# One queue for the later units' transfers, and the next unit's decays turned earlier, in a fused RWKV-6 and SiLU kernel

## The chip, the cores and the metric

The kernel runs on one core of a Trainium2 chip. Its time is the device time of one execution in microseconds (us); the runs below give the median of several executions, and the profile shows one execution of its own, engine by engine. The engines are PE (TensorE, with its weight loads as PEld), DVE (VectorE), ACT (ScalarE), POOL (GpSimd) and SP (SyncE, which here only issues transfers). A "q" behind an engine's name (SPq, ACTq) marks its sequencer: waiting, and issuing transfers.

## The reference

Two blocks follow one another. The first is a linear attention with a decay per channel: for each of 4 batches and 8 heads (48 channels each), over 768 steps,

```python
for t in range(S):
    cur = np.einsum('bhd,bhe->bhde', u[None] * kt, vt)
    y[:, :, t] = np.einsum('bhd,bhde->bhe', rt, state + cur)
    state = wt[:, :, :, None] * state + np.einsum('bhd,bhe->bhde', kt, vt)
```

The second takes the result as 3072 tokens of 384 values: `h = x @ w_in` (384 x 2048), `g = h * sigmoid(h)`, `out = g @ w_out` (2048 x 384). Everything is float32.

## The kernel before, in words

**Units.** The sequence is cut into 6 pieces of 128 steps, the batches into 2 pairs: 12 units, numbered 0 to 11, in the order of time. Unit 5 is the sixth. Within a unit the 128 steps are handled by doubling: at level l (0 to 6) neighbouring blocks of 2^l steps are joined. For this `tw[i][l]` holds the products of w over blocks of 2^l steps; `product` (L404) makes the next level from the one before on POOL, `products_of(i, ...)` names several. `grow_keys` (L624, POOL) and `grow_queries` (L618, DVE) multiply keys and queries by such products, `odd_keys` (ACT) copies keys, `prepare` and `go_on` bundle these for a level, and `burst` (L782) lets PE make the scores of two levels at once. The short distances (below 8 steps) are made apart: `block_bonus` multiplies r, k and w as they lie in DRAM (`tokens_rk`, `tokens_w`) on POOL, `block_sum` adds them up on DVE into `block_sums`, `block_move` sends this to DRAM (`kept`) and reads it back in another layout, and `block_turn` and `block_write` put it into the scores.

**Loads.** `load_blocks(i, name, g)` (L118) loads a quarter of r, k or w of unit i into the room `raw` with four transfers of small runs; a unit has 48 of them, 16 for each of r, k and w. From unit 4 on there is one room per name (`slot`, L99), so the next unit's part can only be loaded once `turn` (L347, on DVE a transpose in blocks, L361) has read the room: w, k and r are turned at different places. `load_rk` loads `tokens_rk` (parts 0 and 1) and `tokens_w` (part 2), `load_values` loads v.

**Second block.** It lags behind the first. In turn i of the loop PE works through `downs(i - 2)`, seven quarters of the down projection (`quarter`, L1298; each accumulates 16 rows of matmuls, and its result is read out of PSUM by ACT at L1328 or by DVE at L1331), and `ups(i - 1)`, twenty parts of the up projection (`first_part`, L1189, matmuls at L1180, joined by DVE at L1207 and ACT at L1201, L1204 and L1223). The quarters 0, 2, 4 and 6 share one bank in PSUM, and so do 3 and 5; each must have been read before the next one adds to it. `sums` (L1282, DVE at L1294) makes the sums that the quarters multiply, `sums_of_x` (L1128) those of the input x.

**x.** After `y_state` (L831) and `y_values` PE has the unit's y; ACT copies it to `yt`. `x_out` (L935) sends it to DRAM (`turned`) in two transfers and `x_in` (L942) reads it back in the layout of tokens: on ACT's queue in the loop.

**Order.** Nothing is scheduled automatically: `mix(i)` (L958) writes the order by hand as a list of groups, each with a number of PE steps (from `downs` and `ups`) that follow it. What is emitted first on an engine or a queue runs first, and a waiting instruction holds up all behind it. For i > NPAIR = 4 the order is the one from L1019 on; unit 5 has another place for two bundles (`soon`). The loads of the next unit are added to the groups at the end of `mix` (L1054 to L1059): k and w early, then v and r. In that order `turn` of w stands in group 9 with products 0 to 3, and products 4 to 6 in group 19; for unit 5, w is turned at the end of turn 4 (`turns`) and multiplied at the start of turn 5 (`start`).

Of the kernel before, what the change touches and what calls it, by code (L numbers as in the profile page):

```python
# [8 lines left out]
F32 = mybir.dt.float32  # L9
# [29 lines left out]
def kernel(  # L39
# [11 lines left out]
    nc = tc.nc  # L51
# [3 lines left out]
    L = 128  # L55
    NL = 7
# [3 lines left out]
    Q = NB * NP  # L60
# [8 lines left out]
    NPAIR = 4  # L69
# [333 lines left out]

    def product(i, l, engine=nc.gpsimd):  # L404
        t = tw[i][l]
        up = pt.tile([128, Q, L >> (l + 1)], F32, name=f"tw{l + 1}", bufs=2 if l == NL - 1 else 1)
        engine.tensor_tensor(out=up, in0=t[:, :, 0::2], in1=t[:, :, 1::2], op=ALU.mult)  # L407
        tw[i].append(up)

# [542 lines left out]
    def both(fn, i, *args):  # L952
        return [(fn, i, b, *args) for b in range(NB)]

    def block_loads(i, names="wkr"):
        return [(load_blocks, i, name, g) for name in names for g in range(4)]

    def mix(i):  # L958
# [15 lines left out]
        def start(j):  # L974
            return [*at(j <= NPAIR + 1, *products_of(j, *range(1, NL))), (grow_own, j, 1)]

        def products_of(j, *ls):
            return [(product, j, l) for l in ls]
# [16 lines left out]
        else:  # L995
            j = i - 1
            if i <= NPAIR:
# [15 lines left out]
                          ([], 1),  # L1013
                          ([(burst, i, 5), (keep_level, i, 5, 0), (keep_level, i, 6, 0), (go_on, i, 6), (block_turn, i), (block_write, i, 1)], 2),
                          ([(keep_level, i, 5, 1), (keep_level, i, 6, 1)], 1),
                          ([(block_write, i, 0)], 1),
                          (end[0], 2), (end[1], 0)]
            else:
                soon = i > NPAIR + 1  # L1019
                keys_2 = [(odd_keys, i, 2), (grow_keys, i, 2, False), *at(soon, (grow_queries, i, 2)), *sum_steps(i, 2)]  # L1020
# [22 lines left out]

        if i == NPAIR:
# [5 lines left out]
        if i < NPAIR:  # L1050
            behind = [group for group, _ in groups[8:]]
            for at, group in enumerate(behind):
                group += loads[at * len(loads) // len(behind):(at + 1) * len(loads) // len(behind)]
        elif ahead:  # L1054
            blocks = block_loads(i + 1, "wkr" if i <= NPAIR else "kwr")
            for at, some in ((1, blocks[0:3]), (2, blocks[3:6]), (3, blocks[6:8]), (12, [(load_values, i + 1), *blocks[8:9]]),
                             (13, blocks[9:10]), (14, blocks[10:11]), (15, blocks[11:])) if i > NPAIR else ((0, blocks[0:3]), (1, blocks[3:6]), (2, [*blocks[6:8]]), (3, [(load_values, i + 1)]),
                             (12, blocks[8:9]), (13, blocks[9:10]), (14, blocks[10:11]), (15, blocks[11:])):
                groups[at][0].extend(some)  # L1059
        return groups  # L1060

# [420 lines left out]
```

## Time and profile before

| what | value |
|---|---|
| median of 3 runs | 577.57 us |
| lowest and highest | 576.17 and 579.52 us |
| the profiled execution | 578.62 us, of which the span of the engines is 576.8 |
| mean granted TensorE clock | 0.997 |
| transfers on SP's queue (q1) | 196272 packets, 44.01 MB |
| transfers on ACT's queue (q10) | 10128 packets, 12.39 MB |
| packets below 512 B | 186048 of 206485 |

A row of the timeline reads: start and length in us, engine, line of the kernel, operation, tile written <- tiles read, shape, count; in brackets the idle time of the engine just before it and what ended it. Starts are counted from the start of the span. Rows of the same kind that follow one another are merged.

### The profile page before, as it was taken

Reading aid. Unit: us, or ns where it says so; the run is one execution under the profiler, and the core shown is the slowest. Engines: PE = TensorE matmul, PEld = TensorE weight load, DVE = VectorE, ACT = ScalarE, POOL = GpSimd, SP = SyncE. Lnnn points to the kernel's source line nnn. Section 1 sums busy time; section 2 is a strip of 40 time slices with the busy share of each in tenths; the row PEclk is TensorE's granted clock in tenths of the full one; section 3 lists DMA queues with packets and bytes.
Section 4 is the critical chain, followed back from the end, with each engine's and each line's share of the span. In section 5 each row is a group of like instructions: output and inputs, shape, how many; then the busy total and the mean of one; then the engine's idle time right before and its main releaser. Section 6 shows DMA issues by size and latency. Waiting matters only on the chain.

```text
span 576.8 us, 18839 instructions
## 1 busy us (share of the span) xinstructions
PE 558.9 (97%) x7782; PEld 518.0 (90%) x7782; DVE 482.5 (84%) x748; ACT 270.8 (47%) x604; POOL 394.8 (68%) x447
## 2 busy tenths in 40 slices
PE   8989999999999899899999999999999999999997
PEld 7767777698899899799999999999999999899997
DVE  7979789898899998799799899999888899782250
ACT  5779694432541372273274273274264272371330
POOL 6998868547799997787687697687696687700000
PEclk9999999999999999899999999999999999999999
DMA  9946885345344453554555555555555553102000
GB/s 222 311 74 186 233 248 94 46 65 126 96 87 75 108 86 68 108 90 82 89 110 96 109 83 98 102 96 91 103 87 96 112 89 71 37 4 56 28 8 21
DMA packets 206485, 57.59 MB, mean 100 GB/s; under 512 B 186048, under 2 KB 198208, under 8 KB 206400
## 3 DMA queue, kind: packets, MB, share of 16 engines
q1 hardware_dynamic: 196272, 44.01, 39.4%
q10 hardware_dynamic: 10128, 12.39, 8.3%
q8 instruction: 61, 1.00, 0.8%
q14 instruction: 24, 0.20, 0.1%
HBM read 47.14 MB, written 9.18 MB: 98 GB/s over the span
## 4 chain that ended last, share of the span: by engine, by line
PE 49%; DVE 15%; SPq 13%; DMA 9%; POOL 7%; issue 4%; ACT 2%; ACTq 0%; DVEq 0%; POOLq 0%
PE p_o L1323 14%; SPq L127 11%; PE p_o L1180 11%; PE p_h L1180 7%; PE p_h L1073 4%; PE p_m L1262 4%; DVE temps L1294 3%; PE p_sc L697 2%; POOL tk L639 2%; DMA raw<-in_k_dram 2%; PE p_h L1323 2%; POOL w_in_sb L260 2%; DVE tr L621 2%; DMA kept<-block_sums 2%; DMA raw<-in_r_dram 1%
## 5 line engine op out<-in xcount | busy, mean ns | idle before, releaser
L639 POOL TENSOR_TENSOR tk<-tk,tw 128x256 f32<-128x256 f32 x128 | 105.0, 841 | 18.3 <-ACT tk L609 8.0
L1323 PE MATMUL p_o<-own,temps 128*128 128x192 f32 x528 | 88.8, 327 | 1.2 <-ACT partial L1328 1.1
L1323 PEld LDWEIGHTS p_o<-own,temps 128*128 128x128 f32 x528 | 85.8, 190 | 2.6 <-ACT partial L1328 2.2
L407 POOL TENSOR_TENSOR tw<-tw 128x256 f32<-128x256 f32 (+6 forms) x83 | 45.4, 546 | 48.2 <-DVE tw L361 44.3
L1180 PE MATMUL p_o<-xt,w_in_sb 128*64 128x128 f32 x1152 | 72.3, 273 | 1.0 <-POOL w_in_sb L1119 0.7
L1073 PE MATMUL p_h<-xt,w_in_sb 128*128 128x256 f32 x288 | 66.1, 384 | 1.7 <-POOL w_in_sb L260 1.6
L1323 PE MATMUL p_o<-w_out_sb,gt 128*128 128x192 f32 x340 | 62.1, 337 | 4.3 <-DVE ob L1331 3.5
L1180 PEld LDWEIGHTS p_o<-xt,w_in_sb 128*64 128x64 f32 x1152 | 64.7, 137 | 1.5 <-POOL w_in_sb L1119 0.9
L1073 PEld LDWEIGHTS p_h<-xt,w_in_sb 128*128 128x128 f32 x288 | 53.6, 190 | 10.0 <-POOL w_in_sb L260 2.4
L1323 PEld LDWEIGHTS p_o<-w_out_sb,gt 128*128 128x128 f32 x340 | 56.5, 194 | 6.6 <-DVE ob L1331 5.1
L490 POOL TENSOR_TENSOR ruk<-tokens_rk 128x384 f32<-128x384 f32 x48 | 53.6, 1138 | 4.2 <-DMA tokens_rk<-in_k_dram 4.2
L621 DVE TENSOR_TENSOR tr<-tr,tw 128x512 f32<-128x512 f32 x61 | 54.1, 886 | 0.7
L1328 ACT COPY partial<-p_o 128x192 f32<-128x192 f32 x33 | 10.4, 319 | 80.4 <-PE p_o L1323 43.8
L1294 DVE TENSOR_TENSOR temps<-gt 128x512 f32<-128x512 f32 (+1 forms) x48 | 44.7, 969 | 0.0
L609 ACT COPY tk<-tk 128x256 f32<-128x256 f32 x52 | 20.9, 403 | 38.7 <-POOL tk L639 30.5
L648 POOL TENSOR_TENSOR tk<-tk,tw 128x256 f32<-128x256 f32 x32 | 25.2, 820 | 16.1 <-DVE tk L361 16.1
L1204 ACT ACTIVATE gt<-p_o 128x512 f32<-128x512 f32 x45 | 26.0, 601 | 19.8 <-PE p_o L1180 19.8
L715 DVE COPY_PREDICATED score<-mask,p_sc 128x512 f32<-128x512 int8 x42 | 31.3, 800 | 0.8 <-PE p_sc L697 0.6
L1328 ACT COPY ob<-p_o 128x192 f32<-128x192 f32 x11 | 3.5, 319 | 59.8 <-PE p_o L1323 53.8
L1323 PE MATMUL p_o<-w_out_sb,temps 128*128 128x192 f32 x176 | 30.4, 326 | 0.0
L490 POOL TENSOR_TENSOR spare<-tokens_rk 128x384 f32<-128x384 f32 x24 | 29.0, 1221 | 0.6
L1323 PE MATMUL p_h<-w_out_sb,gt 128*128 128x192 f32 x168 | 29.1, 326 | 0.0
(240 smaller groups left out, 1293.3 us busy)
## 6 DMA issues: line engine op xcount, KB each, us to landing
w_out_sb<-in_moe_w_in_dram SPq DMA_DIRECT2D x6, 768.0 KB, 6.6
w_out_sb<-in_moe_w_out_dram SPq DMA_DIRECT2D x4, 768.0 KB, 5.9
own<-in_moe_w_out_dram SPq DMA_DIRECT2D x4, 768.0 KB, 6.3
tokens_w<-in_w_dram SPq DMA_DIRECT2D x8, 384.0 KB, 4.6
turned<-yt ACTq DMA_DIRECT2D x16, 192.0 KB, 2.6
xt<-turned ACTq DMA_DIRECT2D x8, 384.0 KB, 3.8
tokens_rk<-in_r_dram ACTq DMA_DIRECT2D x7, 384.0 KB, 4.8
tokens_rk<-in_k_dram ACTq DMA_DIRECT2D x7, 384.0 KB, 6.0
```

The source lines that it names most:

```text
L127: nc.sync.dma_start(out=room[(2 * e + a) * 32:(2 * e + a + 1) * 32, :, g, 0:d1 - d0], in_=src[b0:b0 + NB, e::2, t0:t0 + 32, d0:d1].rearran ...
L407: engine.tensor_tensor(out=up, in0=t[:, :, 0::2], in1=t[:, :, 1::2], op=ALU.mult)
L490: mul = lambda out, one, two: nc.gpsimd.tensor_tensor(out=out, in0=one, in1=two, op=ALU.mult)
L621: nc.vector.tensor_tensor(out=odd, in0=odd, in1=tw[i][l][:, :, 0::2][:, :, :, None].to_broadcast([128, Q, L >> (l + 1), c]), op=ALU.mult)
L639: nc.gpsimd.tensor_tensor(out=out, in0=have, in1=odd_products(i, l, b, *blocks), op=ALU.mult)
L648: nc.gpsimd.tensor_tensor(out=have, in0=have, in1=odd_products(i, l, b, [2, NP * ni]), op=ALU.mult)
L715: nc.vector.copy_predicated(out=dst, mask=masks[l][:, :, None].to_broadcast([128, NB, NP, ni, c]), data=sc[e].rearrange("p (b q) (i c) -> ...
L1073: nc.tensor.matmul(p_h[:, a, :], lhsT=w_in_sb[:, c, f * 128:(f + 1) * 128], rhs=xt[i][:, c, :], start=(a == 0 and c == 0), stop=(a == 1 an ...
L1180: nc.tensor.matmul(p[h:h + PD, q, :], lhsT=left[:, f:f + PD], rhs=right, start=first and q == 0, stop=q == 3, skip_group_check=True)
L1204: nc.scalar.activation(out=g(f, t), in_=have, func=AF.Silu)
L1294: nc.vector.tensor_tensor(out=out, in0=one, in1=two, op=op)
L1323: nc.tensor.matmul(p, lhsT=left(f), rhs=right[:, f, :], start=which in (0, 1, 3) and f == 0, stop=f == FH - 1, skip_group_check=True)
```

## The change

For turns 5 to 11 it does four things, and one at the end of turn 4.

1. The transfers of `x_out`, `x_in` and of `tokens_rk`, five in a turn, are issued by SP and no longer by ACT.
2. The block loads are written into the groups: w first (groups 0 and 1, behind `x_out` and `x_in`), k in groups 2 to 4, r in groups 7, 11, 14 and 15, v in group 12. `block_move` is split: `block_sums` is sent out in group 6, ahead of `tokens_rk`, and read back in group 8; `tokens_w` is loaded in group 10.
3. The next unit's w is turned in groups 6 and 8 and no longer in group 9, its products 0 to 2 are made in group 8 ahead of `go_on(i, 4)`, and products 3 to 6 in group 9 behind it, so that none is left in group 19. As this overlaps with products of the unit at work, the odd units put levels 5 and 6 in the rooms `both_b` and `diag0`, whose last use is earlier.
4. Unit 5 gets the order of the others: the bundle `keys_2` (with `grow_queries(i, 2)`) in group 2 and `keys_3` in group 3.
5. For unit 5 w is turned in the last but two group of turn 4, behind `block_write`, and all its products follow in the next group, behind `block_bonus` 0 to 3.

```diff
     def product(i, l, engine=nc.gpsimd):
         t = tw[i][l]
-        up = pt.tile([128, Q, L >> (l + 1)], F32, name=f"tw{l + 1}", bufs=2 if l == NL - 1 else 1)
+        if i > NPAIR and i % 2 and l + 1 in (5, 6):
+            up = pt.tile([128, Q, L >> (l + 1)], F32, name={5: "both_b", 6: "diag0"}[l + 1], bufs=1)
+        else:
+            up = pt.tile([128, Q, L >> (l + 1)], F32, name=f"tw{l + 1}", bufs=2 if l == NL - 1 else 1)
...
-            return [*at(j <= NPAIR + 1, *both(turn, j, "w"), (product, j, 0)), *both(turn, j, "k")]
+            return [*at(j <= NPAIR, *both(turn, j, "w"), (product, j, 0)), *both(turn, j, "k")]
...
-            return [*at(j <= NPAIR + 1, *products_of(j, *range(1, NL))), (grow_own, j, 1)]
+            return [*at(j <= NPAIR, *products_of(j, *range(1, NL))), (grow_own, j, 1)]
...
-                          ([(block_write, i, 0)], 1),
-                          (end[0], 2), (end[1], 0)]
+                          ([(block_write, i, 0), *at(i == NPAIR, *both(turn, i + 1, "w"))], 1),
+                          ([*end[0], *at(i == NPAIR, *products_of(i + 1, *range(NL)))], 2), (end[1], 0)]
...
-                groups = [([*both(turn, i, "r"), (grow_own, i, 0), (x_out, j)], 2),
-                          ([*at(j >= NPAIR, (add_update, j)), *start(i), *bonus_steps(i, 4), (x_in, j), (reverse_v, i)], 1),
-                          ([*at(not soon, (grow_queries, i, 2)), *at(soon, *keys_2)], 1),
-                          ([*at(soon, *keys_3), *at(not soon, *keys_2), (sums_of_x, j, 0, 1)], 1),
-                          ([(sums_of_x, j, 2), *at(not soon, *keys_3), *bonus_steps(i, 6, 7), (sums_of_x, j, 3, 4, 5, 6)], 2),
+                groups = [([*both(turn, i, "r"), (grow_own, i, 0), (x_out, j, nc.sync), *loads("w", 0, 1)], 2),
+                          ([*at(j >= NPAIR, (add_update, j)), *start(i), *bonus_steps(i, 4), (x_in, j, nc.sync), *loads("w", 2, 3), (reverse_v, i)], 1),
+                          ([*keys_2, *loads("k", 0, 1)], 1),
+                          ([*keys_3, (sums_of_x, j, 0, 1), *loads("k", 2)], 1),
+                          ([(sums_of_x, j, 2), *bonus_steps(i, 6, 7), (sums_of_x, j, 3, 4, 5, 6), *loads("k", 3)], 2),
                           ([(burst, i, 3), *sum_steps(i, 3), (keep_level, i, 3), *sum_steps(i, 4)], 2),
-                          ([*at(ahead, (load_rk, i + 1, (0, 1), nc.scalar)), (block_move, i, False), (block_move, i, True), *at(ahead, (load_rk, i + 1, (2,)))], 1),
-                          ([], 1),
-                          ([(keep_level, i, 4)], 2),
-                          ([(go_on, i, 4), *at(ahead, *both(turn, i + 1, "w"), *products_of(i + 1, 0, 1, 2, 3))], 1),
-                          ([], 1),
-                          ([], 1),
-                          ([], 1),
+                          ([(block_move, i, False), *at(ahead, (load_rk, i + 1, (0, 1)), (turn, i + 1, 0, "w"))], 1),
+                          ([*loads("r", 0)], 1),
+                          ([(block_move, i, True), *at(ahead, (turn, i + 1, 1, "w"), *products_of(i + 1, 0, 1, 2)), (keep_level, i, 4)], 2),
+                          ([(go_on, i, 4), *at(ahead, *products_of(i + 1, 3, 4, 5, 6))], 1),
+                          ([*at(ahead, (load_rk, i + 1, (2,)))], 1),
+                          ([*loads("r", 1)], 1),
+                          ([*at(ahead, (load_values, i + 1))], 1),
                           ([(sums_of_x, j, 7)], 1),
-                          ([(prepare, i, 5)], 2),
-                          ([], 1),
+                          ([(prepare, i, 5), *loads("r", 2)], 2),
+                          ([*loads("r", 3)], 1),
...
-                          ([*at(ahead, *bonus_steps(i + 1, 1, 2, 3)), *at(ahead and i > NPAIR, *products_of(i + 1, 4, 5, 6))], 2),
+                          ([*at(ahead, *bonus_steps(i + 1, 1, 2, 3)), ], 2),
```

`loads(name, *gs)` is `[(load_blocks, i + 1, name, g) for g in gs if ahead]`. The block loads at the end of `mix` stay for turn 4 alone.

More of the change, by code (lines that the diff above doesn't have):

```diff
@@ L1015, in mix @@
                           ([(keep_level, i, 5, 1), (keep_level, i, 6, 1)], 1),
-                          ([(block_write, i, 0)], 1),
-                          (end[0], 2), (end[1], 0)]
-            else:
-                soon = i > NPAIR + 1
-                keys_2 = [(odd_keys, i, 2), (grow_keys, i, 2, False), *at(soon, (grow_queries, i, 2)), *sum_steps(i, 2)]
+                          ([(block_write, i, 0), *at(i == NPAIR, *both(turn, i + 1, "w"))], 1),
+                          ([*end[0], *at(i == NPAIR, *products_of(i + 1, *range(NL)))], 2), (end[1], 0)]
+            else:
+                keys_2 = [(odd_keys, i, 2), (grow_keys, i, 2, False), (grow_queries, i, 2), *sum_steps(i, 2)]
@@ L1021, in mix, with loads @@
                 keys_3 = [(prepare, i, 3), *bonus_steps(i, 5)]
-                groups = [([*both(turn, i, "r"), (grow_own, i, 0), (x_out, j)], 2),
-                          ([*at(j >= NPAIR, (add_update, j)), *start(i), *bonus_steps(i, 4), (x_in, j), (reverse_v, i)], 1),
-                          ([*at(not soon, (grow_queries, i, 2)), *at(soon, *keys_2)], 1),
-                          ([*at(soon, *keys_3), *at(not soon, *keys_2), (sums_of_x, j, 0, 1)], 1),
-                          ([(sums_of_x, j, 2), *at(not soon, *keys_3), *bonus_steps(i, 6, 7), (sums_of_x, j, 3, 4, 5, 6)], 2),
-                          ([(burst, i, 3), *sum_steps(i, 3), (keep_level, i, 3), *sum_steps(i, 4)], 2),
-                          ([*at(ahead, (load_rk, i + 1, (0, 1), nc.scalar)), (block_move, i, False), (block_move, i, True), *at(ahead, (load_rk, i + 1, (2,)))], 1),
-                          ([], 1),
-                          ([(keep_level, i, 4)], 2),
-                          ([(go_on, i, 4), *at(ahead, *both(turn, i + 1, "w"), *products_of(i + 1, 0, 1, 2, 3))], 1),
-                          ([], 1),
-                          ([], 1),
-                          ([], 1),
+                def loads(name, *gs):
+                    return [(load_blocks, i + 1, name, g) for g in gs if ahead]
@@ L1054, in mix @@
         elif ahead:
[L1055 to L1058, printed above, removed]
+            blocks = block_loads(i + 1)
+            for at, some in ((0, blocks[0:3]), (1, blocks[3:6]), (2, [*blocks[6:8]]), (3, [(load_values, i + 1)]),
+                             (12, blocks[8:9]), (13, blocks[9:10]), (14, blocks[10:11]), (15, blocks[11:])) if i <= NPAIR else ():
                 groups[at][0].extend(some)
```

## The prediction

> **What bounds the kernel now.** I read the busy line first, then the stretches of the loop, then the idle marks of PE, and last the queues behind them.
>
> ```profile
> span 576.8 us, 18839 instructions
> PE 558.9 (97%) x7782; PEld 518.0 (90%) x7782; DVE 482.5 (84%) x748; ACT 270.8 (47%) x604; POOL 394.8 (68%) x447
> ```
>
> PE is busy 97% of the span, so the prize is small: at most the time in which PE waits. The change touches turns 5 to 11 of the loop over units and the end of turn 4 (the sixth unit is number 5). I cut the span where PE starts y_state of the unit before (the first L840 row of each turn).
>
> ```profile
> 258.47 0.34 PE L840 MATMUL p_m<-tr,state 48*48 48x128 f32 x4
> ```
>
> ```profile
> 210.99:258.47 47.48, 44.65 (x693) 42.97 (x689) 41.44 (x63) 21.00 (x53) 37.69 (x44) 0.96 0.49 87
> 258.47:301.26 42.79, 42.65 (x692) 41.52 (x689) 39.05 (x61) 19.83 (x51) 32.75 (x38) 1.00 0.52 94
> 301.26:344.03 42.77, 42.77 (x692) 41.49 (x688) 39.20 (x61) 20.57 (x52) 33.92 (x38) 1.00 0.53 96
> 344.03:387.67 43.64, 43.01 (x693) 41.47 (x689) 40.91 (x61) 20.43 (x52) 32.30 (x38) 1.00 0.54 99
> 387.67:430.96 43.29, 42.97 (x693) 41.47 (x689) 39.52 (x61) 20.16 (x51) 34.46 (x39) 1.00 0.52 95
> 430.96:473.52 42.56, 42.20 (x677) 40.92 (x673) 37.77 (x60) 20.18 (x52) 30.80 (x37) 1.00 0.54 98
> ```
>
> These are turns 5 to 10: length, then the busy time of PE, PEld, DVE, ACT and POOL. Turns 5 to 9 hold the same matmuls, yet turn 5 is 4.7 us longer, and turn 8 0.9. Inside a turn the place where PE comes late is the last of the seven quarters of the down projection, which may not start before DVE has read an earlier quarter out of PSUM (L1331, `ob`).
>
> ```profile
> 233.41 4.55 PE L1323 MATMUL p_o<-w_out_sb,gt 128*128 128x192 f32 x16 [2.60 <-DVE ob L1331]
> ```
>
> ```profile
> 277.63 2.76 PE L1323 MATMUL p_o<-w_out_sb,gt 128*128 128x192 f32 x16
> ```
>
> ```profile
> 320.66 2.87 PE L1323 MATMUL p_o<-w_out_sb,gt 128*128 128x192 f32 x16
> ```
>
> ```profile
> 364.26 2.87 PE L1323 MATMUL p_o<-w_out_sb,gt 128*128 128x192 f32 x16
> ```
>
> ```profile
> 450.75 2.76 PE L1323 MATMUL p_o<-w_out_sb,gt 128*128 128x192 f32 x16
> ```
>
> ```profile
> 493.05 2.87 PE L1323 MATMUL p_o<-w_out_sb,gt 128*128 128x192 f32 x16 [0.92 <-DVE ob L1331]
> ```
>
> Counted from the start of its turn this quarter starts at 22.42 (turn 5), 19.16 (6), 19.40 (7), 20.23 (8) and 19.79 (10). Turn 6 has it earliest; turn 7 has the shortest rest, 42.77 - 19.40 = 23.37. A turn without any wait would take 19.16 + 23.37 = 42.53 (estimate). Over that lie 0.26 in turn 6, 0.24 in 7, 1.11 in 8, 0.76 in 9; turn 10, with fewer matmuls, is 19.79 - 19.16 = 0.63 late, and turn 11 shows 0.92 of idle. That is 3.9 us in all, and 4.95 more in turn 5.
>
> What makes it late:
>
> ```profile
> 353.49 0.43 PE L1323 MATMUL p_o<-own,temps 128*128 128x192 f32 x1 [0.53 <-ACT partial L1328]
> ```
>
> ```profile
> 309.69 0.32 ACT L1328 COPY partial<-p_o 128x192 f32<-128x192 f32 x1 [3.86 <-DMA raw<-in_r_dram]
> ```
>
> ```profile
> 354.34 1.30 DVE L361 STREAM_TRANSPOSE tr<-raw 128x512 f32<-128x512 f32 x2 [0.96 <-DMA raw<-in_r_dram]
> ```
>
> ```profile
> 441.41 1.30 DVE L361 STREAM_TRANSPOSE tr<-raw 128x512 f32<-128x512 f32 x2 [1.47 <-DMA raw<-in_k_dram]
> ```
>
> First, ACT stands still behind its own transfers (x_out, x_in): in turn 7 it is idle 3.86 us before a copy out of PSUM, in turn 8 such a copy holds PE 0.53. Secondly, DVE waits for the last loads of r: 0.96 in turn 8, 1.47 in turn 10. Both lead to the late quarter.
>
> **The change part by part.**
>
> *r sooner, on SP.* Today SP issues r last:
>
> ```profile
> 297.35 11.45 SPq L127 DMA_DIRECT2D raw<-in_r_dram  x16
> ```
>
> ```profile
> 318.24 8.42 SPq L127 DMA_DIRECT2D raw<-in_w_dram  x16
> ```
>
> ```profile
> 327.72 0.41 SPq L549 DMA_DIRECT2D kept<-block_sums  x1
> 334.27 0.38 SPq L554 DMA_DIRECT2D spare<-kept  x1
> ```
>
> ```profile
> 341.54 8.72 SPq L127 DMA_DIRECT2D raw<-in_r_dram  x12
> ```
>
> ```profile
> 303.46 2.37 ACT L866 COPY yt<-p_m 48x512 f32<-48x512 f32 x4 [0.18 <-PE p_m L861]
> ```
>
> From 328.13 to 334.27 SP stands 6.1 us before the read of `kept`, and r goes behind that. The change puts the loads of tokens_rk and a quarter of r into this hole and splits the rest of r over the turn. At 8.42 / 16 = 0.53 us per load, SP's new order is: x_out once y is copied (305.83, 4.6 us into turn 7), with the loads of w queued behind that wait and behind x_in's wait for `turned`; then w and x_in 9 us, k 8.5, two outputs and `kept` (ready only 26 us in, as now), tokens_rk and r 3, the five reads of `kept` 3, w's tokens, values and the other twelve r 10: the last r is out about 44 us in, against 51 today (twelve by 350.26, four more behind, turn 7 from 301.26). The waits of DVE for r go (estimate: all). SP's added work is five transfers a turn, 5 x 0.53 = 2.6 us. They hide in that hole; if `kept` still lands 6.5 us after its issue, half of the hole stays, and SP loses its slack: the first rival below.
>
> *ACT freed.* x_out, x_in and two loads leave ACT, and with them the waits of its copies. PE's 0.53 in turn 8 goes, and its like in turn 10. x_in now stands behind eight loads of w, about 10 us into the turn; first used by DVE at 318.67 - 301.26 = 17.4:
>
> ```profile
> 318.67 0.81 DVE L1141 TENSOR_TENSOR xt<-xt 128x256 f32<-128x256 f32 x1
> ```
>
> The Trainium skill, "DMA: Bandwidth & Descriptors", section "Issuing engines are not separate DMA queues", speaks against this part: it says that all issuers share the same 16 engines, and that issuing from several only saves issue time, usually small. By it, taking ACT's queue away would only lose issue time; the 3.86 us row above shows a cost of the second queue that the section does not count, so I follow the row.
>
> *w turned in groups 6 and 8, its products ahead of go_on(4).* DVE does the same two transposes earlier, in gaps before L1207. On POOL the products now come before the keys of levels 4 and 5 (the fourth product waits there for DVE's go_on(4), with those keys behind it only from level 5 on; the rooms of both_b and diag0 have no reader left, so they add no wait):
>
> ```profile
> 329.15 1.33 DVE L715 COPY_PREDICATED score<-mask,p_m 128x512 f32<-128x512 int8 x2
> ```
>
> ```profile
> 332.34 2.65 POOL L407 TENSOR_TENSOR tw<-tw 128x512 f32<-128x512 f32 x4 [5.58 <-DVE tw L361]
> 334.95 1.20 POOL L639 TENSOR_TENSOR tk<-tk,tw 128x256 f32<-128x256 f32 x2
> ```
>
> ```profile
> 336.92 0.69 PE L697 MATMUL p_sc<-tr,tk 48*64 48x64 f32 x32
> ```
>
> POOL was idle 5.58 us before the products. The second half of w now takes the place of L715 on DVE and is turned by 329.15 + 0.65 = 329.8, 2.5 us sooner. The seven products (2.65 + 2.06, the latter from the row below) and two pairs of keys (1.20 each) then end by 336.9, today 336.15. PE needs these keys for the second half of its scores, 0.5 us after 336.92. Cost 0, at worst 0.3 a turn. At the end of a turn three products leave POOL,
>
> ```profile
> 346.94 2.06 POOL L407 TENSOR_TENSOR tw<-tw 128x32 f32<-128x32 f32 x3
> ```
>
> 2.06 us beside DVE's sums, which helps turn 11, where no r is awaited.
>
> Turns 6 to 11 together: I take 0.2 + 0.2 + 1.1 + 0.7 + 0.6 + 0.9 = 3.7 of the 3.9; bounds 0 and 3.9.
>
> *The sixth unit.*
>
> ```profile
> 212.09 1.49 DVE L1294 TENSOR_TENSOR temps<-gt 128x512 f32<-128x512 f32 x1
> ```
>
> ```profile
> 219.07 0.69 DVE L1294 TENSOR_TENSOR temps<-gt,temps 128x512 f32<-128x512 f32 x1
> 219.68 1.30 DVE L361 STREAM_TRANSPOSE tw<-raw 128x512 f32<-128x512 f32 x2
> 220.90 1.26 DVE L361 STREAM_TRANSPOSE tk<-raw 128x512 f32<-128x512 f32 x2
> ```
>
> ```profile
> 221.06 1.04 POOL L407 TENSOR_TENSOR tw<-tw 128x512 f32<-128x512 f32 x1 [3.77 <-DVE tw L361]
> ```
>
> ```profile
> 230.69 1.13 DVE L527 TENSOR_REDUCE block_sums<-ruk 128x4 f32<-128x192 f32 x4 [1.85 <-POOL ruk L490]
> ```
>
> ```profile
> 308.64 1.30 DVE L361 STREAM_TRANSPOSE tk<-raw 128x512 f32<-128x512 f32 x2
> ```
>
> ```profile
> 320.24 0.36 DVE L1331 TENSOR_TENSOR ob<-p_o,partial 128x192 f32<-128x192 f32 x1
> ```
>
> The turn of w only swaps places with the sums of L1294 on a DVE that has no gap there, so k is still turned at 222.16. What goes is the 1.85 of idle. What comes ahead of `ob` is prepare(3). Turn 7 has the new order already and takes 320.60 - 309.94 = 10.66 from the turn of k to `ob`, 10.3 without its wait for r; so `ob` ends at 222.2 + 10.3 = 232.5 instead of 233.36, a gain of 0.9. Against it: the products now run beside the sums, which take 1.49 beside a busy POOL and 0.69 alone; four of them by 0.8 would be 3.2. Ends: -0.9 and +2.3; I take -0.5, near turn 7's row. The gap in front of the quarter stays over 2 us, and with it the half clock:
>
> ```profile
> 235.00:238.00 3.00, 3.00 (x15) 2.57 (x17) 2.01 (x5) 0.00 (x1) 2.92 (x5) 0.53 0.40 49
> ```
>
> The quarter took 4.55 instead of 2.76, 1.8 more. Whether a somewhat shorter gap still costs this is open; I leave it in the sum.
> The Trainium skill, "TensorE: Matmul & The Clock Gate", section "What's actually happening", has the clock halved only after an idle window of about 3.4 us, free-running. By it a gap of 2.6 us would go unpunished; here it did not, so no gain is taken from it.
>
> **Sum.** -3.7 - 0.5 = -4.2. The profiled execution took 578.62 (span 576.8 and 1.8 around it), 1.05 over the median of 577.57. Span 572.6, and against the median 573.4.
>
> **Rivals.**
> - *SP becomes the bound* (slower). SP's row from 297.35 to 341.54 is 44.2 long with 6.1 of hole: 38 of issuing, plus 2.6. If r's loads keep their 0.72 (11.45 / 16) and half of the hole stays, a turn of SP is 40.6 + 3.1 = 43.7 and more, over 42.53. It decides from the point where x_in lands later than 17.4 us into the turn; the margin of about 4 us is used up in three turns, then each of four turns costs 1 to 2: +3 to +7 with few waits removed, 580.6. For: 0.72 is measured. Against: r's slow issues stand where ACT issues too. Chance 0.16.
> - *Hidden anyway.* DVE is 92% busy in the turns, so `ob` may stay as late by its own work; then only ACT's waits go, 0.53 and its like, about 1 us: 576.6. Chance 0.22.
> - *The sixth unit loses its wait wholly*, with the half clock: 2.6 + 1.8 instead of 0.5: 569.5. It needs `ob` 3 us sooner than DVE's work allows by the rows. Chance 0.12.
>
> **Numbers.** A measurement of this kernel tells about 0.5% (2.9 us) from no change. The forecast, 573.4, has 0.50, of which 0.07 lies above 574.7. Faster: 0.43 + 0.12 + 0.02 = 0.57; same 0.27; slower 0.16. The range goes from 570.3 (3.9 and the sixth unit's -0.9 and -1.8, with run-to-run spread) to 579.0, cutting half of the first rival and part of the third.
>
> **What would show it.** Right: no idle mark of DVE before the turn of r, none of ACT behind a transfer, the last quarter 19.2 us into turns 6 to 10, turns near 42.5, turn 5 still near 47. Wrong: SP's x_out row starting later turn by turn; POOL's L639 rows ending after 337 in turn 7's terms with PE waiting at L697; DVE idle at L1141 for x_in; turn 5 near 43.

## The result and the profile after

| what | before | after |
|---|---|---|
| median of 7 runs | 577.57 us (576.17 to 579.52) | 574.25 us (573.2 to 574.72) |
| the profiled execution | 578.62 us, span 576.8 | 573.2 us, span 571.4 |
| mean granted TensorE clock in it | 0.997 | 1.0 |

The ratio of the runs is 0.994, with a 95% interval of 0.9922 to 0.9958: faster by 0.6%. The forecast was 573.4. Every ratio below stands against runs of the kernel before on the same chip, and below 1 is faster. Disturbed executions are left out of the ratios, but the median and the profile of the kernel with eight more transfers on SP include such ones.

The page of the kernel after, its span, its busy line, the two transfer queues and the shares of the chain that ended last:

```profile
span 571.4 us, 18874 instructions
...
PE 555.4 (97%) x7782; PEld 517.3 (91%) x7782; DVE 481.7 (84%) x748; ACT 270.8 (47%) x604; POOL 394.3 (69%) x447
...
q1 hardware_dynamic: 203712, 54.23, 46.1%
q10 hardware_dynamic: 2688, 2.16, 1.5%
...
PE 73%; DVE 11%; POOL 4%; DMA 4%; SPq 3%; issue 3%; ACT 1%; DVEq 0%; POOLq 0%
```

The last of these lines for the kernel before:

```profile
PE 49%; DVE 15%; SPq 13%; DMA 9%; POOL 7%; issue 4%; ACT 2%; ACTq 0%; DVEq 0%; POOLq 0%
```

About 10 MB went from ACT's queue (q10) to SP's (q1). PE is as busy as before in per cent, which tells little. The chain tells more: SP's queue fell from 13% to 3% of it and the DMAs from 9% to 4%, and PE took their place. The stretches of the kernel after, turns 5 to 11, cut and read as in the prediction (length, then the busy time of PE, PEld, DVE, ACT, POOL; granted clock third from the end):

```profile
211.37:257.04 45.67, 42.70 (x693) 41.52 (x689) 42.36 (x63) 20.85 (x53) 40.24 (x47) 1.00 0.50 92
257.04:299.47 42.43, 42.43 (x692) 41.54 (x688) 39.03 (x61) 20.50 (x52) 32.81 (x38) 1.00 0.52 98
299.47:341.90 42.43, 42.43 (x692) 41.54 (x688) 39.00 (x61) 20.47 (x52) 32.80 (x38) 1.00 0.54 99
341.90:384.34 42.44, 42.44 (x693) 41.55 (x689) 39.03 (x61) 20.51 (x52) 32.84 (x38) 1.00 0.53 98
384.34:426.77 42.43, 42.43 (x692) 41.54 (x688) 39.01 (x61) 20.50 (x52) 32.81 (x38) 1.00 0.53 98
426.77:468.58 41.81, 41.81 (x677) 40.97 (x673) 38.40 (x61) 19.89 (x51) 32.19 (x38) 1.00 0.52 98
468.58:510.40 41.82, 41.35 (x642) 40.20 (x640) 36.76 (x59) 18.24 (x43) 23.30 (x27) 1.00 0.18 39
```

The last turn of the kernel before, not shown so far:

```profile
473.52:515.79 42.27, 41.35 (x642) 40.20 (x640) 37.18 (x59) 18.73 (x44) 25.62 (x30) 1.00 0.20 41
```

Four turns have the same length to 0.01 us, with PE busy throughout: by this profile nothing else sets them any more. The seven turns together fell from 304.80 to 299.03, by 5.77; the part before turn 5, which the change leaves alone, is 0.38 longer in this execution (211.37 against 210.99), and so the span fell by 5.4.

What is left of the waits at the quarter, in the timeline of PE of the kernel after:

```profile
233.66 0.92 PE L1328 MATMUL p_o<-w_out_sb,gt 128*128 128x192 f32 x4 [2.97 <-DVE ob L1336]
...
487.65 1.57 PE L1328 MATMUL p_o<-w_out_sb,gt 128*128 128x192 f32 x8 [0.47 <-DVE ob L1336]
```

These are turns 5 and 11. (Lines have moved by 3 or 5: L1323 is L1328 now, L1331 is L1336.) SP's queue in the turn that begins at 299.47:

```profile
302.87 2.15 SPq L942 DMA_DIRECT2D turned<-yt  x2
305.11 4.71 SPq L127 DMA_DIRECT2D raw<-in_w_dram  x8
309.93 0.39 SPq L948 DMA_DIRECT2D xt<-turned  x1
310.36 3.94 SPq L127 DMA_DIRECT2D raw<-in_w_dram  x8
314.40 8.43 SPq L127 DMA_DIRECT2D raw<-in_k_dram  x16
...
324.75 0.33 SPq L552 DMA_DIRECT2D kept<-block_sums  x1
325.17 0.54 SPq L158 DMA_DIRECT2D tokens_rk<-in_r_dram  x1
325.76 0.59 SPq L158 DMA_DIRECT2D tokens_rk<-in_k_dram  x1
326.40 2.73 SPq L127 DMA_DIRECT2D raw<-in_r_dram  x4
329.24 0.40 SPq L557 DMA_DIRECT2D spare<-kept  x1
...
339.95 3.91 SPq L127 DMA_DIRECT2D raw<-in_r_dram  x8
```

The hole between `kept` and its read-back is filled with `tokens_rk` and a quarter of r, and the last r is out at 343.86, 44.4 into the turn. In the table of waits over turns 6 to 11, SP's wait for `kept` is, before and then after (us in total, times, longest):

```profile
SPq L554 <- DMA kept<-block_sums: 27.8, 6, 6.1
```

```profile
SPq L557 <- DMA kept<-block_sums: 1.2, 1, 1.2
```

### The profile page after: what moved, and what is told of

Its sections match the earlier page's. It is cut to its first block, busy times and chain, and to the rows that moved or that the text cites. A ratio compares the mean times of both kernels' runs of the same rounds, so it can differ in the third digit from the quotient of the medians.

```text
span 571.4 us, 18874 instructions
## 1 busy us (share of the span) xinstructions
PE 555.4 (97%) x7782; PEld 517.3 (91%) x7782; DVE 481.7 (84%) x748; ACT 270.8 (47%) x604; POOL 394.3 (69%) x447
## 3 DMA queue, kind: packets, MB, share of 16 engines
HBM read 47.14 MB, written 9.18 MB: 99 GB/s over the span
## 4 chain that ended last, share of the span: by engine, by line
PE 73%; DVE 11%; POOL 4%; DMA 4%; SPq 3%; issue 3%; ACT 1%; DVEq 0%; POOLq 0%
PE p_o L1328 25%; PE p_o L1185 15%; PE p_h L1185 10%; PE p_h L1078 5%; PE p_h L1328 4%; PE p_m L1267 4%; PE p_sc L700 2%; PE p_m L864 2%; SPq L127 2%; POOL tk L642 2%; DVE score L718 2%; PE p_m L843 1%; DVE tr L624 1%; PE p_m L700 1%; DMA tokens_w<-in_w_dram 1%
## 5 line engine op out<-in xcount | busy, mean ns | idle before, releaser
L642 POOL TENSOR_TENSOR tk<-tk,tw 128x256 f32<-128x256 f32 x112 | 92.6, 846 | 7.8 <-DVE tw L410 3.8
L1328 PE MATMUL p_o<-own,temps 128*128 128x192 f32 x528 | 88.1, 327 | 0.2 <-DVE temps L1299 0.2
L1328 PEld LDWEIGHTS p_o<-own,temps 128*128 128x128 f32 x528 | 86.0, 190 | 0.5 <-DVE temps L1299 0.5
L1328 PE MATMUL p_o<-w_out_sb,gt 128*128 128x192 f32 x340 | 60.1, 330 | 4.1 <-DVE ob L1336 3.4
L410 POOL TENSOR_TENSOR tw<-tw 128x256 f32<-128x256 f32 (+6 forms) x71 | 39.6, 558 | 33.0 <-DVE tw L361 29.4
L1328 PEld LDWEIGHTS p_o<-w_out_sb,gt 128*128 128x128 f32 x340 | 55.2, 190 | 5.6 <-DVE ob L1336 4.0
L624 DVE TENSOR_TENSOR tr<-tr,tw 128x512 f32<-128x512 f32 x57 | 51.6, 905 | 0.7
L651 POOL TENSOR_TENSOR tk<-tk,tw 128x256 f32<-128x256 f32 x32 | 24.7, 806 | 27.5 <-DVE tk L361 27.5
L1328 PE MATMUL p_o<-w_out_sb,temps 128*128 128x192 f32 x176 | 30.4, 326 | 0.0
L1328 PE MATMUL p_h<-w_out_sb,gt 128*128 128x192 f32 x168 | 29.1, 326 | 0.0
```

The source lines that it names most:

```text
L624: nc.vector.tensor_tensor(out=odd, in0=odd, in1=tw[i][l][:, :, 0::2][:, :, :, None].to_broadcast([128, Q, L >> (l + 1), c]), op=ALU.mult)
L642: nc.gpsimd.tensor_tensor(out=out, in0=have, in1=odd_products(i, l, b, *blocks), op=ALU.mult)
L651: nc.gpsimd.tensor_tensor(out=have, in0=have, in1=odd_products(i, l, b, [2, NP * ni]), op=ALU.mult)
L1328: nc.tensor.matmul(p, lhsT=left(f), rhs=right[:, f, :], start=which in (0, 1, 3) and f == 0, stop=f == FH - 1, skip_group_check=True)
```

## The experiments

### The parts, each alone on the kernel before

**Only the queue**: x_out, x_in and tokens_rk to SP, the order as it was.

```diff
-  groups = [([..., (x_out, j)], 2),
-            ([..., (x_in, j), (reverse_v, i)], 1),
+  groups = [([..., (x_out, j, nc.sync)], 2),
+            ([..., (x_in, j, nc.sync), (reverse_v, i)], 1),
...
-            ([*at(ahead, (load_rk, i + 1, (0, 1), nc.scalar)), (block_move, i, False), ...], 1),
+            ([*at(ahead, (load_rk, i + 1, (0, 1))), (block_move, i, False), ...], 1),
```

> The kernel before, with x_out, x_in and the two loads of tokens_rk issued by SP; nothing else. Theory (r must come sooner, and that is the order on SP): x_out now stands behind the last loads of r, 8 to 9 us into the turn, r still lands last, DVE still waits 0.4 to 1.5 us for it; turns 6 to 10 stay between 42.8 and 44, time 576.5 to 579. Rival (freeing ACT is enough): turns at 42.4, 573.5 to 574.5.

Measured: 590.46, ratio 1.0228 (1.0172 to 1.0283). Both expectations fell: this part alone costs 2.3%. SP's queue of this kernel in a turn that begins at 302.38:

```profile
301.28 9.36 SPq L127 DMA_DIRECT2D raw<-in_r_dram  x14
310.74 0.88 SPq L939 DMA_DIRECT2D turned<-yt  x2
314.12 0.38 SPq L945 DMA_DIRECT2D xt<-turned  x1
...
334.27 0.54 SPq L549 DMA_DIRECT2D kept<-block_sums  x1
339.03 0.38 SPq L554 DMA_DIRECT2D spare<-kept  x1
```

The loads of r of the turn before still run when the turn begins, so x_out leaves at 310.74, 8.4 into the turn. SP then stands 2.5 us before x_in and 4.2 before the read-back of `kept`. DVE's waits of the same kernel, and what PE makes of it:

```profile
DVE spare L560 <- DMA spare<-kept: 11.5, 4, 3.5
```

```profile
346.53 1.10 PE L1180 MATMUL p_o<-xt,w_in_sb 128*64 128x128 f32 x16 [2.06 <-DVE p_o L1207]
```

DVE waits for the read-back, comes late to the up projection's joins, and PE with it. In turns 6 to 11 DVE also waits 5.6 us for loads of w and 2.9 for loads of r, so the wait that the theory named is there, beside larger ones. Part of the 11.4 us by which this profile's span is longer is the clock: two waits of PE of about 2 us (at 346.53 and 483.54) were followed by 6.83 and 3.41 us at a granted clock of 0.5, which is at most 5.1 us of lost work (estimate, half of the sum). This is the first rival of the prediction, *SP becomes the bound*. Its mechanism is real, but it bites at `block_turn` and at the loads of w and r, and not at x_in.

**Only the order**: the new load order and the moved bundles of turn 5, but the five transfers on ACT, w turned as before, also for the sixth unit.

```diff
...
-  ([*both(turn, i, "r"), (grow_own, i, 0), (x_out, j)], 2),
+  ([*both(turn, i, "r"), (grow_own, i, 0), (x_out, j), *loads("w", 0, 1)], 2),
...
+  ([(block_move, i, False), *at(ahead, (load_rk, i + 1, (0, 1), nc.scalar))], 1),
+  ([*loads("r", 0)], 1),
+  ([(block_move, i, True), (keep_level, i, 4)], 2),
...
```

> The changed kernel with ACT issuing its five transfers again, w late for all units and the sixth unit's w as before: what stays is the order of the loads on SP (and the places of the bundles in turn 5). Theory: DVE waits for r no longer; ACT still holds the third quarter 0 to 1.6 us in some turns and turn 5 stays at 47.5 to 48.5: 576.0 to 578.0, no gain that can be told. Rival (the order alone makes the gain): 574.0 to 575.0.

Measured: 578.7, ratio 1.0013 (0.9998 to 1.0028), no gain, 0.7 over the theory's range. DVE waits for no load of r any more, but ACT still stands at x_out: in turns 6 to 11 it is idle 12.2 us before copies of `partial` where the profile names `turned<-yt` as the end of the wait, and 10.9 where it names `raw<-in_w_dram`. Turns 6 to 11 are 1.4 shorter than before in all, turn 5 is 48.53, 1.05 longer.

**Only the sixth unit**: w of unit 5 turned in turn 4, and the bundles moved.

```diff
-  return [*at(j <= NPAIR + 1, *both(turn, j, "w"), (product, j, 0)), *both(turn, j, "k")]
+  return [*at(j <= NPAIR, *both(turn, j, "w"), (product, j, 0)), *both(turn, j, "k")]
...
-  ([(block_write, i, 0)], 1), (end[0], 2), (end[1], 0)]
+  ([(block_write, i, 0), *at(i == NPAIR, *both(turn, i + 1, "w"))], 1),
+  ([*end[0], *at(i == NPAIR, *products_of(i + 1, *range(NL)))], 2), (end[1], 0)]
...
-  soon = i > NPAIR + 1
+  soon = True
...
```

> The kernel before with the sixth unit's part alone: w turned and multiplied in turn 4, the bundles of keys as for the other units. Theory: the last quarter of turn 5 starts 22.3 into the turn as before, DVE's idle 1.85 goes but prepare(3) comes ahead; 0 to 1.5 us less than before by whether the half clock comes, 576.0 to 577.9; turns 7 to 10 as before. Rival (the sixth unit is half of the gain or more): 575.9 or less.

Measured: 577.89, ratio 1.0006 (0.999 to 1.0023), no gain, at the upper end of the theory's range. Turn 5 is 45.73 in its profile, without a halved clock, but turn 6 takes 43.65 and turn 10 43.45 (42.79 and 42.56 before), which the theory did not have. Turn 10 has this wait:

```profile
459.26 0.55 PE L1183 MATMUL p_o<-gt,in_sum 128*64 128x128 f32 x6 [1.42 <-DVE p_o L1210]
```

### All parts but one

**Without the sixth unit's early w**:

```diff
-  return [*at(j <= NPAIR, *both(turn, j, "w"), (product, j, 0)), *both(turn, j, "k")]
+  return [*at(j <= NPAIR + 1, *both(turn, j, "w"), (product, j, 0)), *both(turn, j, "k")]
...
-  ([(block_write, i, 0), *at(i == NPAIR, *both(turn, i + 1, "w"))], 1),
-  ([*end[0], *at(i == NPAIR, *products_of(i + 1, *range(NL)))], 2), (end[1], 0)]
+  ([(block_write, i, 0)], 1),
+  (end[0], 2), (end[1], 0)]
```

> The changed kernel, with the sixth unit's w turned and multiplied where it was before (turn of w at the end of turn 4 with k, product 0 there, products 1 to 6 at the start of turn 5). Theory (the gain is in turns 6 to 11, the sixth unit gives little): turns 6 to 10 stay at 42.4 (turn 10 41.8); in turn 5 DVE waits about 2 us for POOL at the block sums and reads the quarter about 0.8 us later (23.0 us into the turn instead of 22.2), so 0.5 to 1.5 us more than the changed kernel, 574.5 to 575.8, plus 1.5 where the half clock comes. Rival (the sixth unit is where the gain is): the time goes back to 577 or more.

Measured: 576.01, ratio 0.9963 (0.9951 to 0.9974): 1.8 us over the kernel after by the medians, 0.2% by the ratios, and inside the theory's range for an execution with the half clock, which its profile has. Turns 6 to 11 agree with the kernel after within 0.01. Turn 5 is 48.50 and has a second wait, because the moved bundles crowd ACT and DVE while w is still in the way:

```profile
228.96 0.76 PE L1328 MATMUL p_o<-w_out_sb,temps 128*128 128x192 f32 x3 [1.29 <-ACT partial L1333]
```

**Without the queue**: the five transfers back on ACT.

```diff
-  (x_out, j, nc.sync) ... (x_in, j, nc.sync) ... (load_rk, i + 1, (0, 1))
+  (x_out, j) ... (x_in, j) ... (load_rk, i + 1, (0, 1), nc.scalar)
```

> The changed kernel, with x_out, x_in and the two loads of tokens_rk back on ACT; the order of the loads and of w stays. Theory: DVE does not wait for r, but ACT stands behind its own transfers again and holds the third quarter by 0 to 0.7 us; turns 6 to 10 between 42.4 and 43.1, time 574.3 to 576.3. Rival (freeing ACT is nearly all): turns 42.8 to 43.6, 576.5 to 577.5.

Measured: 576.21, ratio 0.9975 (0.996 to 0.9989), inside the theory's range at its upper end. The profiled execution took 578.16, 2 us over the median; its turn 7 takes 44.17, where the theory had 43.1 at most. ACT in that turn, and PE behind it:

```profile
308.71 2.96 ACTq L942 DMA_DIRECT2D turned<-yt  x2
311.72 0.32 ACT L1333 COPY partial<-p_o 128x192 f32<-128x192 f32 x1 [5.45 <-DMA turned<-yt]
```

```profile
312.09 0.76 PE L1328 MATMUL p_o<-own,temps 128*128 128x192 f32 x3 [1.46 <-ACT partial L1333]
```

**Without turning w sooner in the later units** (the sixth unit keeps its early w):

```diff
-  ([(block_move, i, False), *at(ahead, (load_rk, i + 1, (0, 1)), (turn, i + 1, 0, "w"))], 1),
+  ([(block_move, i, False), *at(ahead, (load_rk, i + 1, (0, 1)))], 1),
...
-  ([(block_move, i, True), *at(ahead, (turn, i + 1, 1, "w"), *products_of(i + 1, 0, 1, 2)), (keep_level, i, 4)], 2),
-  ([(go_on, i, 4), *at(ahead, *products_of(i + 1, 3, 4, 5, 6))], 1),
+  ([(block_move, i, True), (keep_level, i, 4)], 2),
+  ([(go_on, i, 4), *at(ahead, *both(turn, i + 1, "w"), *products_of(i + 1, 0, 1, 2, 3))], 1),
...
-  ([*at(ahead, *bonus_steps(i + 1, 1, 2, 3)), ], 2),
+  ([*at(ahead, *bonus_steps(i + 1, 1, 2, 3), *products_of(i + 1, 4, 5, 6))], 2),
```

> The changed kernel, with w of the next unit turned in group 9 and multiplied in groups 9 (0 to 3) and 19 (4 to 6) as before, for units 6 and on; the order on SP stays. Theory: PE does not notice, turns 6 to 9 at 42.4 to 42.6, turn 11 0.3 longer; 574.0 to 575.2. Rival (turning w sooner is what pays): turns 6 to 9 near 43, time 576.5 or more.

Measured: 573.98, ratio 0.9919 (0.9894 to 0.9944), the kernel after's time. Its turns are 42.43 and 41.81 as well, and turn 11 is 41.57 where the kernel after has 41.82; the theory had it longer. The third part of the change brings nothing that can be told.

### The two halves of ACT's transfers

From the kernel after, x_out and x_in alone went back to ACT, and in another kernel tokens_rk alone.

```diff
-  (x_out, j, nc.sync) ... (x_in, j, nc.sync)
+  (x_out, j) ... (x_in, j)
```

> The changed kernel with x_out and x_in alone back on ACT; the loads of tokens_rk stay on SP. Theory (it is x_out and x_in that hold ACT's copies of the quarters): turns 6 to 10 between 42.4 and 44 as in e3, 575.5 to 576.8. Rival (it is the loads of tokens_rk): turns at 42.4, 574.0 to 574.6.

Measured: 573.98, ratio 0.9944 (0.9929 to 0.9959). Turns 6 to 11 are those of the kernel after. The theory fell: x_out and x_in on ACT cost nothing measurable once the order is the new one. ACT does still stand for transfers, 9.2 us in four waits of turns 5 to 11, none longer than 2.8, but only one of the copies behind them holds PE (0.83 us in turn 5, at 221.28), and that turn is 45.68, as in the kernel after.

```diff
-  (load_rk, i + 1, (0, 1))
+  (load_rk, i + 1, (0, 1), nc.scalar)
```

> The changed kernel with the two loads of tokens_rk alone back on ACT; x_out and x_in stay on SP. Theory: turns 6 to 10 at 42.4, 573.9 to 574.6. Rival: the loads of tokens_rk hold ACT's copies of the up projection, turns 42.8 to 43.5, 575.5 or more.

Measured: 575.23, ratio 0.9959 (0.9945 to 0.9974), between the theory's times and the rival's. No copy of ACT waits for a transfer from turn 5 on, and turns 7 to 10 are 42.43 and 41.81. The profiled execution lies 1.9 above the kernel after's, and turn 5 is 1.98 longer, all of it behind the quarter, where PE works without a stop and the clock was halved for one window (below). That is not all: the two executions with a granted clock of 1.0 took 574.16 and 574.22, those of the kernel after 573.2 to 573.53. No trace of these two is kept, so where their 0.7 us are stays open.

The two halves do not add up. Against the kernel after's 0.994, the ratio is higher by 0.04% with x_out and x_in on ACT, by 0.2% with tokens_rk and by 0.35% with both; only the last is clear of the intervals. ACT stands at x_out with x_out and x_in alone as well, but shorter (2.8 us at most, 5.45 with both). What it waits for there is in the last section.

### How much room SP has

w's second half is loaded twice, eight more transfers a turn; the second load brings the same data.

```diff
-  (x_in, j, nc.sync), *loads("w", 2, 3), (reverse_v, i)], 1),
+  (x_in, j, nc.sync), *loads("w", 2, 3), *loads("w", 2, 3), (reverse_v, i)], 1),
```

> The changed kernel, with two quarters of w loaded twice in turns 5 to 10: eight transfers more a turn on SP, 8 x 0.53 = 4.2 us of issuing, the same data. In the changed kernel SP waits about 4.6 us in a turn. Theory (SP is near its limit, but not over it): the eight take nearly all of that; x_out starts 2 to 4 us later, turns 6 to 10 grow by 0 to 2 us; 574.5 to 582. Rival (SP has room to spare and its order alone mattered): turns stay at 42.4, 574.0 to 574.5.

Measured: 588.17, ratio 1.0148 (1.0113 to 1.0184); the median lies over the theory's range and the rival's. The ratio rests on executions of 583.49 to 588.77, which are 9.2 to 14.5 us over the kernel after's median, 1.5 to 2.4 for each of the six turns with eight more transfers. The profiled execution took 593.97. Its turns 6 to 9 take 47.14, 46.05, 46.93 and 46.75, together 17.1 us more than the kernel after's, but for 17.1 us of them the granted clock was 0.5, which can be up to half of the surplus (estimate). So these turns are no measure of what eight issues cost.

There is little room: in the kernel after the records of SP's issues fill 35.5 of the 42.43 us from one x_out (302.87) to the next, and up to the last r (343.86) SP never stands longer than 0.95. The wait that grows in the profile is again the read-back (DVE, turns 6 to 11):

```profile
DVE spare L563 <- DMA spare<-kept: 15.1, 5, 4.5
```

### Turn 5, where most of the waiting is left

In turn 5 work of DVE was put behind the read of `ob` (the base is the kernel with w late in the later units): sums of the scores, `prepare(3)` and the sums of x go to groups 4 to 11.

```diff
+  if i == NPAIR + 1:
+      own_loads = [[step for step in group if step[0] is load_blocks] for group, _ in groups]
+      for place, steps in {2: [(odd_keys, i, 2), (grow_keys, i, 2, False), (grow_queries, i, 2)], 3: [],
+                           4: [*sum_steps(i, 2), (prepare, i, 3), *bonus_steps(i, 5), (sums_of_x, j, 0, 1), *bonus_steps(i, 6, 7)],
+                           5: [(burst, i, 3), (keep_level, i, 3), (sums_of_x, j, 2, 3), *sum_steps(i, 3)],
...
+                           9: [(go_on, i, 4), ..., (sums_of_x, j, 4)],
```

> The changed kernel with w late as in e4, and in turn 5 alone DVE's work put behind the read of the quarter: block sums 2, prepare(3) and the first sums of x behind it, the other sums of x and the block sums 3 and 4 two to seven groups later, the way through kept accordingly later. Theory (in turn 5 PE waits because DVE has 3 us of work too many ahead of the read): the last quarter starts 19.2 to 19.6 into turn 5, no half clock there, turn 5 between 42.6 and 43.8 instead of 45.7, time 571.0 to 572.5. Rival (the wait is handed on, to POOL's keys or to the joins of the up projection): PE waits 2 to 3 us at the scores or at the up projection, turn 5 stays at 45 or more, 573.5 or more.

Measured: 571.61, ratio 0.9892 (0.9872 to 0.9912), inside the theory's range. The quarter starts 19.22 into turn 5, without a wait, and no half clock follows. The turn takes 44.33, over the theory's 43.8, because one new wait came, for the fifth sum of x, put too late:

```profile
243.29 0.88 PE L1196 MATMUL p_h<-xt,w_in_sb 128*64 128x128 f32 x12 [1.51 <-DVE xt L1168]
```

The next kernel moves that one step from group 9 to group 6.

```diff
-  6: [(load_rk, i + 1, (0, 1))], 7: [],
+  6: [(load_rk, i + 1, (0, 1)), (sums_of_x, j, 4)], 7: [],
...
-  9: [(go_on, i, 4), ..., (sums_of_x, j, 4)],
+  9: [(go_on, i, 4), ...],
```

> e7 with one sum of x (step 4, 0.3 us on DVE) three groups sooner in turn 5. In e7 turn 5 was 44.3 long, with 1.5 us in which PE waited for this sum. Theory (that wait alone is left in turn 5): turn 5 between 42.6 and 43.2, time 569.8 to 570.6. Rival (DVE is late there whatever comes first): another wait of 1 us or more at L1196, 571.2 to 571.8.

Measured: 570.25, ratio 0.9887 (0.9869 to 0.9905), inside the theory's range and the fastest kernel here, 4.0 us below the kernel after by the medians and 0.5% by the ratios. Its turn 5 (the theory had 43.2 at most) and the 0.59 of waiting left in it:

```profile
210.92:254.34 43.42, 42.83 (x692) 41.50 (x688) 42.21 (x63) 20.64 (x53) 38.89 (x44) 1.00 0.51 94
```

```profile
246.21 0.98 PE L1196 MATMUL p_h<-spare,w_in_sb 128*64 128x128 f32 x14 [0.59 <-DVE p_h L1223]
```

## Why the prediction was right, and where it was not

**Turns 6 to 11, -3.7: right.** Measured in the two profiles: 0.36, 0.34, 1.20, 0.86, 0.75 and 0.45, together 3.96. The estimated turn without a wait, 42.53, is 42.43. The quarter starts 19.16 into turns 6 to 10.

**r sooner, on SP: right as a mechanism.** The last r leaves 44.4 into the turn (forecast 44), and no wait of DVE for a load is left in turns 6 to 11. What the prediction did not say is that this alone is worth nothing: the new order without the new queue measured 1.0013.

**ACT freed: right only together with the order.** The new queue without the order costs 2.3%, the order without the queue nothing, both without the early w of the sixth unit gain 0.4%. The order makes the room on SP that the five transfers need. The prediction read ACT's 3.86 us as the cost of x_out and x_in; in the new order these two on ACT cost nothing measurable, and it takes the two loads of tokens_rk beside them. ACT's idle time there is real, but it is not behind x_out: it lies before and between the two issues of x_out, which wait for loads that SP has issued (last section).
On the rule weighed there (the Trainium skill, "DMA: Bandwidth & Descriptors", section "Issuing engines are not separate DMA queues", by which a second issuer only saves issue time, usually small): the kernel with x_out and x_in on ACT agrees with its first half, 0.9944 against 0.994. "Usually small" does not hold for the sum of them here: SP's issues fill 35.5 us of a turn of 42.43, and five more without the new order cost 2.3%.

**w sooner in the later units, 0: right.** Without it the time is the same. The second pair of keys came in time: no wait of PE at the scores.

**The sixth unit, -0.5: the mis-sized term.** In the profiles turn 5 fell by 1.81, but the start of the quarter only from 22.42 to 22.30. The step that failed is the 10.3 us from the turn of k to `ob`: it took 10.64, and k itself was turned 0.43 later (11.60 into the turn, before 11.17), as the sums beside the products became slower: two of them took 1.27 each, where the prediction's row has 0.69 for one beside an idle POOL. The timeline of DVE of the kernel after has these two, and one of 0.69 when only the small products were left:

```profile
217.68 2.54 DVE L1299 TENSOR_TENSOR temps<-gt 128x512 f32<-128x512 f32 x2
...
221.06 0.69 DVE L1299 TENSOR_TENSOR temps<-gt,temps 128x512 f32<-128x512 f32 x1
```

The rest of the 1.81 is the half clock. The prediction tied it to a gap of over 2 us and left it in the sum. The gap even grew, from 2.60 to 2.97, and the half clock did not come in this execution: that is luck, by the place of the gap among the clock's windows (last section), and no merit of the change. Where it comes, as in the kernel with tokens_rk on ACT, turn 5 takes 47.65, no less than the 47.48 before. The sign "turn 5 still near 47" was thus not seen here, though its cause, the gap, was. The early w is still worth its place: without it the moved bundles make turn 5 48.50.

**Sum.** The profiled execution fell by 5.4 (forecast 4.2): 0.26 more in turns 6 to 11, 1.3 more in turn 5, 0.38 less in the early part. The medians fell by 3.3. The three executions of the kernel after that show a granted clock of 1.0 took 573.2 to 573.5, the four at 0.993 to 0.997 took 574.25 to 574.72, so the profiled execution has no halved window and the median's has about two: one takes 0.003 off the mean (3.41 x 0.5 / 571.4). Where these lay was not kept, so whether the median has the half clock of turn 5 is not shown.

**The rivals.** *SP becomes the bound* did not come, but it was nearer than its chance says: the queue without the order, or eight more transfers, brings it. *Hidden anyway* is out: DVE had the time once r came earlier. *The sixth unit loses its wait wholly* did not come here. The reason given against it, that DVE's work does not allow it by the rows, holds only for this order: with some of that work behind the read of `ob` the quarter starts 19.23 into turn 5, and 570.25 was measured where the rival said 569.5.

## What to carry over

Before a transfer is moved to a queue, count that queue's issue time and its holes over one whole turn: here SP's issues filled 32.4 of the 42.77 us of turn 7 before, with a hole of 6.1, and 35.5 of 42.43 after. The same move cost 2.3% or helped, according to the order of the loads and whether the hole ahead of the read-back had been filled. Parts of a change can each measure zero or worse alone and gain together, so a part is judged by taking it out as well as by doing it alone. Ahead of a wait that sets the path, look at what stands before it on the late engine and is not needed by it: moving that work (570.25) brought 0.5% by the ratios, about as much as the whole change did (0.6%).

## What the runs showed of the hardware

**The half clock goes by windows, not by the gap.** In every profiled execution here where the clock was halved in turn 5, it was for 3.41 us from one fixed raster, whose steps are 3.413 us long and start somewhere between 4.5 and 7.3 us (before, the clock's record starts at 5.71 and the halved window at 234.41, 67 steps later). Stretches of one window each. Before (first the window that holds the gap, then the next; the second number is PE's busy time, the granted clock is third from the end):

```profile
230.99:234.41 3.42, 1.00 (x6) 1.00 (x7) 3.36 (x9) 0.93 (x2) 3.26 (x6) 1.00 0.39 49
234.41:237.82 3.41, 3.41 (x12) 3.05 (x10) 2.60 (x6) 0.00 (x0) 3.33 (x5) 0.50 0.41 51
```

After, the same two windows of its own raster:

```profile
231.94:235.35 3.41, 1.69 (x10) 1.69 (x11) 3.31 (x7) 0.00 (x0) 3.25 (x5) 1.00 0.40 52
235.35:238.77 3.42, 3.42 (x94) 3.13 (x94) 3.42 (x6) 0.34 (x2) 3.27 (x4) 1.00 0.29 91
```

The kernel with tokens_rk on ACT:

```profile
229.99:233.40 3.41, 0.43 (x3) 0.25 (x2) 3.34 (x8) 0.26 (x1) 3.33 (x6) 1.00 0.41 55
233.40:236.81 3.41, 3.41 (x12) 3.41 (x12) 3.38 (x7) 0.00 (x0) 3.33 (x4) 0.50 0.18 20
```

The gap is 2.60 us in the first, 2.97 in the second and 2.98 in the third. The longer one of the kernel after goes unpunished, because the edge of a window cuts it: 1.72 us of idle lie in one window. The almost equal one of the third kernel lies in one window, with 2.98 of idle, and costs: turn 5 takes 47.65 against 45.67. From turn 5 on, the windows with the least idle that were still followed by a halved one held 2.03 and 2.06 (the queue without the order, turns 10 and 7) and 2.08 (the five transfers on ACT, gap 2.24); the most that went unpunished is 1.73 (w late in the later units). So in these stretches the limit lies between 1.73 and 2.03 us of idle in a window. Idle time alone does not set it everywhere: early in the kernel windows with 1.43 and 1.60 of idle were followed by a halved one, in the fastest kernel and in the one with tokens_rk on ACT. This is the first:

```profile
35.20:38.62 3.42, 1.99 (x38) 1.36 (x37) 1.92 (x2) 2.61 (x5) 2.90 (x5) 1.00 0.38 47
38.62:42.03 3.41, 3.41 (x9) 2.69 (x10) 3.34 (x3) 2.99 (x5) 3.28 (x4) 0.50 0.60 115
```

What else counts is open. A gap of 2 to 3 us is a matter of luck with a price: from the start of the quarter to the end of turn 5 it takes 24.99 to 25.35 us in the profiles with the halved window and 23.37 to 23.41 in those without it, 1.6 to 2.0 more. Elsewhere the halved time lasted longer, 6.83 us (the queue without the order) and 10.24 (eight more transfers on SP).
The Trainium skill, "TensorE: Matmul & The Clock Gate", section "What's actually happening", has a free-running window of about 3.4 us, and this raster agrees with it; it has the clock fall after an idle window, and here windows in which PE was busy for 0.43 to 1.99 us were enough.

**A transfer on one queue can hold back the other's issuer.** With all five transfers on ACT, ACT is idle 5.45 us before the copy at 311.72. This time lies before and between the two issues of x_out, and the copy follows 0.04 us after the second. The two issues one by one, each behind a load on SP:

```profile
305.84 1.32 SPq L127 DMA_DIRECT2D raw<-in_w_dram  x1
308.71 0.35 ACTq L942 DMA_DIRECT2D turned<-yt  x1
```

```profile
308.19 0.45 SPq L127 DMA_DIRECT2D raw<-in_w_dram  x1
311.37 0.31 ACTq L942 DMA_DIRECT2D turned<-yt  x1
```

`yt` was complete at 306.27, so y is not what is waited for. The trace records a semaphore (a counter that tells of a landing) for each transfer and each wait. In this kernel the transfers of both queues share eight of them, and the sequencer waits for the last landing on a transfer's semaphore before it issues the transfer. The first issue of x_out has the semaphore of the load issued at 305.84, which landed at 308.64, the second that of the load issued at 308.19, which landed at 311.29: each leaves less than 0.1 us later. So do all twelve issues of x_out in turns 5 to 10 of this kernel, each behind a load of w, and all ten in turns 7 to 11 of the kernel before, each behind a load of r. With only x_out and x_in on ACT the semaphores fall otherwise: in turns 6 to 10 the first issue stands behind a load of r, which SP issues ahead of the loads of w, and ACT's longest wait is 2.8. In the kernel after, on SP, the semaphore had been free for 1.69 us or more at every x_out of turns 5 to 11. So ACT stood for landings of SP's loads that x_out does not need. Why the program gives out the semaphores in just this way is open.
